# Placing attention keys by small DMAs instead of masked products, with eps as a statistics group and a second shape for the normalise step

## The chip, the cores and the metric

The kernel runs on one core of one Trainium2 chip, in one launch. The metric is the device time in microseconds (us), as the median of several runs. A profile is one execution with tracing, and its *span* runs from the first to the last instruction, about 2 us less than the time of the same execution.

Engines in the profile: PE is TensorE's matmul part, PEld its weight load, DVE is VectorE, ACT is ScalarE, POOL is GpSimd, and SP is SyncE, which here issues every DMA of the program. "SPq" is time in which SP's sequencer executes an instruction.

## The reference, cut to what matters

```python
def _A_ref(x, wqkv, wo):                    # S=2048, D=512, 32 heads of 16, window W=256
    qkv = (x @ wqkv).reshape(B, S, 3, H, Dh).transpose(2, 0, 3, 1, 4)
    q, k, v = qkv[0], qkv[1], qkv[2]
    scores = einsum("bhqd,bhkd->bhqk", q, k) * Dh ** -0.5
    p = softmax(where(causal_and_within_window, scores, -1e9))
    return einsum("bhqk,bhkd->bhqd", p, v)... @ wo
def _B_ref(x, w1, b1, w2, b2):              # F=1792, mixes tokens
    u = gelu(einsum("bsd,sf->bdf", _layernorm(x), w1) + b1)
    return (einsum("bdf,fs->bds", u, w2) + b2).transpose(0, 2, 1)

x = A_x
for _ in range(2):                          # written out twice in the reference
    x = x + _A_ref(_layernorm(x), A_wqkv, A_wo)
    x = x + _B_ref(_layernorm(x), B_w1, B_b1, B_w2, B_b2)
```

Each layernorm is (x - mean) / sqrt(var + 1e-5). B receives a normalised x and normalises it again, so there the two are merged into one.

## The kernel before

The kernel first describes its work as a graph of operations. Then it replays a fixed order, a long packed constant `ORDER` that a scheduler made beforehand: it says which operation stands where, and which of several engines does it. Each engine then runs its own operations strictly in that order. An operation waits on semaphores for what it reads:

```python
for o in self.order[e]:                     # one stream for each engine, SP included
    for s, v in waits[o.idx]:
        eng.wait_ge(sem(s), v)
    ins = o.fn(eng, o.cols32) if o.flex else o.fn(eng)
    ins.then_inc(sem(mark[o.idx][0]), 16 if o.dma else 1)
```

So SP is one queue, in order: the transposed activations (`xhT`), the weights `w1b` and `w2b` of the MLP and everything else stand behind each other, each with its own wait.

Four heads of 16 rows are used at a time by the score matmuls, and two heads share the 32 rows of one such matmul (the profile has all 1488 of them as 32*128). Their keys must therefore lie block-diagonally in `kbd`: for each row group r, rows 32r to 32r+15 hold head 0's keys in one half, and rows 32r+16 to 32r+31 hold head 1's keys in the other, with zeros elsewhere. The kernel before makes this with two products by a 0/1 column `par` for each key tile:

```python
op("vector:evk", lambda e: e.tensor_copy(stg[:, ts.slot, 0:n], at()), ...)   # PSUM to SBUF: "staged"
for h in range(2):
    f_kz = lambda e, h=h: e.tensor_scalar(
        dst(h), stg[:, ts.slot, 0:n].rearrange("p (s n) -> p s n", n=64), par[:, h:h + 1], 0.0,
        op0=ALU.mult, op1=ALU.add)
    op("gpsimd:kz", f_kz, reads=[ts, ("par", h)], ..., alts=[("vector", f_kz, ...)])
```

There are 24 such tiles, 12 in each attention layer (the first block of a layer goes another way). The layernorm:

```python
op("vector:stat", lambda e: e.bn_stats(stats[:, t, :], x_sb[:, t, :]), ...)
op("vector:agg",  lambda e: e.bn_aggr(agg[:, t, :], stats[:, t, :]), ...)
...
op("vector:var",  lambda e: e.tensor_scalar(rstd[:, t0:t1, 0], agg[:, t0:t1, 1], a, b, op0=ALU.mult, op1=ALU.add), ...)
op("gpsimd:rstd", lambda e: e.tensor_tensor(rstd..., rstd..., mhalf..., op=ALU.pow), ...)      # to the power -1/2
op("vector:xh",   lambda e: e.tensor_scalar(xh_sb[:, t, :], x_sb[:, t, :], agg[:, t, 0:1], rstd[:, t, :],
                                            op0=ALU.subtract, op1=ALU.mult), ...)               # "normalise"
```

The softmax here doesn't subtract the row's maximum and nothing guards it: scores larger than these inputs give would overflow.

## Time and profile before

| | before |
|---|---|
| median (lowest to highest) | 464.39 us (460.69 to 464.5) |
| span of the profiled run, mean granted clock | 461.1 us, 0.993 |

The first part of the profile page gives each engine's busy time, its share of the span and its instructions. The fourth part follows the last instruction back through what released it, and gives shares of the span.

```profile
PE 419.1 (91%) x6394; PEld 200.9 (44%) x6456; DVE 323.5 (70%) x596; ACT 325.9 (71%) x377; POOL 226.5 (49%) x296
...
PE 60%; ACT 15%; DVE 11%; POOL 7%; issue 3%; DMA 2%; SPq 1%
```

Next come groups of instructions with equal shapes: engine, operation, what is written and read, count | busy us, mean ns | idle time before them and its main releaser.

```profile
L687 ACT ACTIVATE pt<-PS 128x1024 bf16<-128x1024 f32 x292 | 275.7, 1047 | 24.9 <-PE PS L672 24.0
...
L491 DVE TENSOR_SCALAR xh_sb<-x_sb,agg,rstd 128x512 bf16<-128x512 bf16 x64 | 36.9, 594 | 7.3 <-POOL rstd L484 7.1
...
L595 DVE TENSOR_SCALAR kbd<-stg,par 128x512 bf16<-128x512 bf16 x27 | 15.7, 586 | 0.8 <-ACT stg L593 0.7
L595 POOL TENSOR_SCALAR kbd<-stg,par 128x512 bf16<-128x512 bf16 x21 | 15.5, 739 | 0.0
...
L482 DVE TENSOR_SCALAR rstd<-agg 128x2 f32<-128x2 f32 x31 | 8.8, 285 | 0.5
```

The change aims at the last four: the normalise steps, the key products on two engines, and the small eps steps. Single lines can be asked for their shortest, median and longest duration in ns (then first and last start in us). The three here are a load of weights from HBM by SP, the DMA that transposes activations, and the normalise step:

```profile
L777 SPq DMA_DIRECT2D w1b<-in_B_w_dram x112: 340/469/1679, 44.5 to 401.1; - x112
...
L543 SPq DMA_TRANSPOSE xhT<-xh_sb x24: 1189/1197/2607, 18.1 to 314.1; - x24
...
L491 DVE TENSOR_SCALAR xh_sb<-x_sb,agg,rstd x64: 314/409/1890, 5.2 to 391.6; 128x512 bf16<-128x512 bf16 x64
```

For an SPq line the duration is how long the queue is held, not when the data land: a load of `w1b` holds it for 0.47 us in the median and lands 2.7 us after its issue.

### The profile page before, as it was taken

What the parts mean: (1) busy time and instruction counts of PE and PEld (TensorE: products, weight loads), DVE (VectorE), ACT (ScalarE), POOL (GpSimd) and SP (SyncE); (2) the same over time, 40 slices, a digit from 0 to 9 for tenths busy, and PEclk for the clock granted to TensorE, in tenths of its full rate; (3) what the DMA queues carried; (4) which work ended last, traced back from release to release, by engine and by line L of the source; (5) the groups of instructions that cost most, each with busy time, mean ns of one, the idle gap of its engine ahead of it and who ended that gap; (6) DMA issues with size and microseconds to landing.
All of it is one profiled execution on the core that took longest, in us unless ns stands there. A gap on an engine that the chain in (4) does not pass through costs nothing.

```text
span 461.1 us, 14645 instructions
## 1 busy us (share of the span) xinstructions
PE 419.1 (91%) x6394; PEld 200.9 (44%) x6456; DVE 323.5 (70%) x596; ACT 325.9 (71%) x377; POOL 226.5 (49%) x296
## 2 busy tenths in 40 slices
PE   6998787998777999999999999998789999999996
PEld 5654344354223444445445444434344344444442
DVE  6998799859677649755567867798986698431215
ACT  6998789999988960616988898999979962340000
POOL 3668678677866651000466557676956661000000
PEclk9999999999988999999999999999999999999999
DMA  8412521000040347630063132422003238662443
GB/s 255 134 28 44 134 47 37 3 4 1 25 138 1 103 112 192 172 102 1 15 103 106 13 94 47 117 59 72 3 1 82 72 91 234 181 170 58 134 137 127
DMA packets 82463, 39.76 MB, mean 86 GB/s; under 512 B 20960, under 2 KB 82400, under 8 KB 82400
## 3 DMA queue, kind: packets, MB, share of 16 engines
q1 hardware_dynamic: 82400, 38.82, 32.0%
q8 instruction: 51, 0.84, 0.8%
q14 instruction: 12, 0.10, 0.1%
HBM read 33.56 MB, written 2.10 MB: 77 GB/s over the span
## 4 chain that ended last, share of the span: by engine, by line
PE 60%; ACT 15%; DVE 11%; POOL 7%; issue 3%; DMA 2%; SPq 1%
PE PS L514 35%; ACT pt L687 14%; PE PS L842 8%; POOL pt L705 6%; PE PS L672 6%; PE PS L721 5%; PE PS L609 3%; PE PS L516 3%; DVE rl L741 2%; DVE xh_sb L491 2%; ACT kbd L582 1%; DVE kbd L595 1%; POOL rstd L484 1%; DMA xhT<-xh_sb 1%; DVE qT L572 1%
## 5 line engine op out<-in xcount | busy, mean ns | idle before, releaser
L687 ACT ACTIVATE pt<-PS 128x1024 bf16<-128x1024 f32 (+1 forms) x304 | 283.2, 1036 | 24.9 <-PE PS L672 24.0
L705 POOL TENSOR_TENSOR pt<-pt,ldm 128x256 int32<-128x256 int32 (+3 forms) x216 | 170.7, 805 | 89.7 <-ACT pt L687 83.8
L672 PE MATMUL PS<-qT,kbd 32*128 32x256 bf16 (+4 forms) x1488 | 60.4, 252 | 12.3 <-DVE rl L741 3.0
L514 PE MATMUL PS<-xh_sb,w1b 128*128 128x512 bf16 x256 | 65.2, 385 | 4.4 <-issue 2.5
L514 PE MATMUL PS<-uT,w2b 128*128 128x512 bf16 x257 | 63.2, 380 | 1.7 <-issue 1.3
L869 DVE SCALAR_TENSOR_TENSOR x_sb<-PS,b2col,x_sb 128x512 bf16<-128x512 f32 x32 | 23.5, 748 | 49.7 <-PE PS L514 47.5
L484 POOL TENSOR_TENSOR rstd<-rstd,mhalf 128x2 f32<-128x2 f32 (+1 forms) x33 | 23.9, 725 | 63.8 <-DVE rstd L482 62.4
L721 PE MATMUL PS<-pt,vb 64*32 64x320 bf16 (+4 forms) x2976 | 45.4, 253 | 9.0 <-POOL pt L705 5.4
L741 DVE STREAM_TRANSPOSE rl<-PS 128x1024 f32<-128x1024 f32 x32 | 39.7, 1242 | 17.1 <-PE PS L721 16.8
L514 PE MATMUL PS<-xhT,wqkv 128*128 128x512 bf16 (+1 forms) x198 | 46.4, 356 | 5.4 <-ACT pt L687 2.2
L672 PEld LDWEIGHTS PS<-qT,kbd 32*128 32x128 bf16 x1488 | 21.9, 92 | 67.0 <-ACT pt L687 44.7
L857 ACT ACTIVATE uT<-rl,b1col 128x512 bf16<-128x512 f32 x28 | 18.3, 712 | 42.1 <-DVE rl L853 42.1
L468 DVE BATCH_NORM_STATS2 stats<-x_sb 128x6 f32<-128x512 bf16 x64 | 43.0, 681 | 0.5
L491 DVE TENSOR_SCALAR xh_sb<-x_sb,agg,rstd 128x512 bf16<-128x512 bf16 x64 | 36.9, 594 | 7.3 <-POOL rstd L484 7.1
L721 PEld LDWEIGHTS PS<-pt,vb 64*32 64x32 bf16 x2976 | 28.7, 89 | 27.3 <-POOL pt L705 13.9
L514 PE MATMUL PS<-uT,pt 128*128 128x512 bf16 x165 | 39.8, 379 | 0.2
L514 PEld LDWEIGHTS PS<-xh_sb,w1b 128*128 128x128 bf16 x276 | 23.4, 99 | 33.9 <-issue 8.0
L514 PEld LDWEIGHTS PS<-uT,w2b 128*128 128x128 bf16 x270 | 24.4, 98 | 31.5 <-issue 3.6
L842 PE MATMUL PS<-xh_sb,w1b 128*128 128x512 bf16 x165 | 37.1, 379 | 0.2
L609 PE MATMUL PS<-wqkv,xhT 128*64 128x256 bf16 x512 | 36.0, 276 | 0.7 <-DMA xhT<-xh_sb 0.3
L514 PE MATMUL PS<-wo_sb,oT 128*128 128x512 bf16 x109 | 29.1, 394 | 2.0 <-DVE xh_sb L491 1.0
L609 PEld LDWEIGHTS PS<-wqkv,xhT 128*64 128x64 bf16 x512 | 25.0, 109 | 9.6 <-issue 5.1
(66 smaller groups left out, 380.2 us busy)
## 6 DMA issues: line engine op xcount, KB each, us to landing
w1b<-in_B_w_dram SPq DMA_DIRECT2D x112, 128.0 KB, 2.7
w2b<-in_B_w_dram SPq DMA_DIRECT2D x70, 128.0 KB, 2.5
pt<-in_B_w_dram SPq DMA_DIRECT2D x42, 128.0 KB, 3.1
out_dram<-x_sb SPq DMA_DIRECT2D x16, 128.0 KB, 1.8
x_sb<-in_A_x_dram SPq DMA_DIRECT2D x3, 512.0 KB, 7.5
wqkv<-in_A_wqkv_dram SPq DMA_DIRECT2D x4, 256.0 KB, 4.6
wqkv<-in_A_wqkv_dram SPq DMA_DIRECT2D x1, 512.0 KB, 7.0
wo_sb<-in_A_wo_dram SPq DMA_DIRECT2D x1, 512.0 KB, 4.0
```

What stands on the lines that cost most here:

```text
L468: op("vector:stat", lambda e: e.bn_stats(stats[:, t, :], x_sb[:, t, :]), reads=[f"x{t}"], writes=[f"st{t}"], cost=dve_cost(512), after=lat ...
L484: op("gpsimd:rstd", lambda e: e.tensor_tensor(rstd[:, t0:t1, 0], rstd[:, t0:t1, 0], mhalf[:, 0:1].to_broadcast([P, t1 - t0]), op=ALU.pow), ...
L491: f_xh = lambda e: e.tensor_scalar(xh_sb[:, t, :], x_sb[:, t, :], agg[:, t, 0:1], rstd[:, t, :], op0=ALU.subtract, op1=ALU.mult)
L514: return e.matmul(o, lhsT=w, rhs=x, start=start, stop=stop, skip_group_check=True)
L609: last = e.matmul(bank(ft)[64 * j:64 * j + 64, sc * 256:(sc + 1) * 256], lhsT=xhT[:, tx.slot, c, tok:tok + 64], rhs=wqkv[:, c, 1024:1536]. ...
L672: last = e.matmul(bank(tt[r // 2], r % 2)[:, base + c0 * 64:base + (c0 + n) * 64], lhsT=kbd[32 * r:32 * r + 32, tk.slot, o, jj].rearrange( ...
L687: op("scalar:exp", lambda e, ts=ts, tp=tp, i=i, cols=cols: e.activation(probs(tp)[:, i, 0:cols, :], pair(ts)[:, :, 0:cols].rearrange("p r ...
L705: return e.tensor_tensor(v, v, m, op=ALU.mult)
L721: last = e.matmul(bank(t, h)[32 * r:32 * r + 32, i + q0 * 64:i + (q0 + n) * 64], lhsT=vb[64 * h:64 * h + 64, tk.slot, jj, 4 * o + r, :], r ...
L741: op("vector:od", lambda e, t=tod, tr=tr: e.transpose(rl[:, tr.slot:tr.slot + 2].rearrange("p a b -> p (a b)"), pair(t)), reads=[(tod, i) ...
L842: last = e.matmul(bank(tu, tt), lhsT=v()[:, sc - b0, k0 + tt * P:k0 + (tt + 1) * P], rhs=xh_sb[:, sc, :], start=(sc == b0), stop=(sc == NT ...
L869: op("vector:resy", lambda e: e.scalar_tensor_tensor(x_sb[:, t, :], bank(ft), b2col[:, t:t + 1], x_sb[:, t, :], op0=ALU.add, op1=ALU.add), ...
```

## The change

The intent is to relieve VectorE and GpSimd. A DMA can place the keys, since the off-diagonal zeros stay where they are once written. Eps becomes a third group of statistics, so the aggregate already contains it and the eps step falls away. And half of the normalise steps write 513 elements as three rows of 171, a shape that is meant to keep them from waiting for GpSimd. A new order comes with it, which is not readable as text.

```diff
+        for i in range(1, 3):
+            op("gpsimd:zk", lambda e, i=i: e.memset(kbd[:, i].bitcast(dt.float32), 0.0), reads=["mhalf"], writes=["zk"], ...)
...
-                for h in range(2):
-                    f_kz = lambda e, h=h: e.tensor_scalar(dst(h), stg[...], par[:, h:h + 1], 0.0, ...)
-                    op("gpsimd:kz", f_kz, ..., alts=[("vector", f_kz, ...)])
+                def f_kz(e):
+                    got = []
+                    for h in range(2):
+                        for r in range(4):
+                            p = 32 * r + 16 * h
+                            got.append(e.dma_start(kbd[p:p + 16, tk.slot, o, a // 64:b // 64, h, :],
+                                                   stg[p:p + 16, ts.slot, 0:n].rearrange("p (s n) -> p s n", n=64)))
+                    return got
+                op("sync:kz", f_kz, reads=[ts, "zk"], ..., cost=1500, issue=2000.0, dma=True, parts=8, prio=-2e5)
...
-            op("vector:var", ...)                                   # the eps step
+        op("vector", lambda e: e.memset(stats[:, :, :, 6:9], 0.0), writes=["eps0"])
+        for i, c in enumerate((EPS, EPS * EPS / (1.0 + EPS))):
+            op("vector", lambda e, i=i, c=c: e.memset(stats[:, i, :, 8], D * c), ...)
...
+            def f_xh1(e):                                           # 32 of the 64 normalise steps
+                return e.tensor_scalar(xh_pad[:, t, 0:D + 1].rearrange("p (a b) -> p a b", a=3), x_pad[:, t, 0:D + 1],
+                                       agg[:, t, 0:1], rstd[:, t, :], op0=ALU.subtract, op1=ALU.mult)
...
-    bias=b1col[:, ft:ft + 1], scale=1.0),
+    bias=b1col[:, ft:ft + 1], scale=(1.0 + EPS) ** -0.5),
```

The scheduler's note for a whole group of eight DMAs is `issue=2000.0`, that is 2.0 us of SP.

## The prediction

> **What bounds the kernel now.** No single engine. The busy table gives TensorE 419 of 461 us (91%), ScalarE 326, VectorE 324, GpSimd 227. In the MLP stretches (170 to 215, 381 to 409 us) TensorE is busy 99%. In the two attention layers (9 to 170, 216 to 377 us) the exponentials start every 0.92 us at best: 40 of them need 37 us, and the groups of 40 take 39.7 to 44.8, so ScalarE is nearly full; VectorE is too in places (35 of 40 us from 40 to 80, 37 of 40 from 300 to 340, where TensorE idles 6 to 8 us). The chain of waits says the same: PE 60%, ACT 15%, DVE 11%, POOL 7%. TensorE's idle time, 42 us, caps the gain.
>
> **What the change removes.** The key products: 27 on VectorE (15.7 us, 586 ns each), 21 on GpSimd (15.5 us); 33 epsilon steps on VectorE (9.1 us). The new order takes a net 6 evictions from ScalarE (0.6 us each). The normalise step has minimum 314, median 409, mean 594 and maximum 1890 ns: such a tail is a wait. [...]
>
> **What it adds.** 192 DMAs of 16 partitions, in 24 groups of eight, on the one SP queue; two zero fills of about 1.9 us; 9 instead of 6 statistics per aggregate (166 ns, near unchanged). A plain issue takes 332 to 469 ns in the trace, so I estimate 2.7 to 3.5 us per group, 72 us in all. SP waited some 300 us before, so it has room, but it is in order. The packets are 128 B; 256 B ones took 18 ns, so moving them costs about 5% of the DMA engines: no limit.
>
> **How much is critical.** VectorE sheds about 20 us plus lock waits, GpSimd 14. Most is off the chain: its "normalise" and "key product" pieces were 3% (14 us). ScalarE sheds 3 to 4 us in its full stretches. Gain: 8 to 12 us. Against it: a key tile now passes staging (0.7), eight issues (3) and landing (2), about 6 us, where the order leaves 5 to 7 us of TensorE work between the key matmuls and the first scores in about four places: 2 to 4 us of score stalls. Net about 8 us: **456.5 us**, 8 in 10 between 448 and 464. Faster by over 2%: 0.40; within 2%: 0.55; slower by over 2%: 0.05.
>
> **What would show it.** VectorE busy near 300 us, GpSimd near 210; [...]groups of 40 exponentials falling toward 39 us; eight issues per key tile near 3 us; a few waits of score matmuls on the key DMA, up to 2 us; MLP stretches unchanged.
>
> **What would make it wrong.** Issues of 16-partition DMAs costing clearly more than 0.4 us, which delays transposes and weight loads behind them; or far less, when the gain reaches 12 us. The new order removing stalls beyond those named, such as the 3.6 us wait for a weight load at 442 us and the half-clock spell at 143 us.

The sum is: 8 to 12 us gained, 2 to 4 lost in score stalls, net about 8 and so 456.5 us. The "lock waits" stand in it, without a figure of their own.

What those waits are the trace before does show. The 24 normalise steps with no GpSimd operation beside them take 314 to 414 ns. Of the 40 others, 17 take 367 to 416 ns and 23 take 509 to 1890, and each of these 23 ends 0.15 us after the end of a mask or key product on GpSimd.

## More of the kernel before

TensorE is busy for 91% of the span, and DMA is almost absent from the chain: hardly any data is waited for.

No plain copy between two on-chip buffers stands in this trace. The view of waits for SP, then the one for all other engines (total us, times, longest):

```profile
SPq L777 <- PE PS L672: 85.5, 6, 49.6
```

```profile
PEld PS L514 <- DMA w2b<-in_B_w_dram: 0.6, 1, 0.6
```

SP is mostly waiting: the line shown, its largest, is weight loads that wait for their buffer. And TensorE practically never waits for a DMA: the second line is its largest such wait.

## The result, and the profile after

| | before | after |
|---|---|---|
| median of 4 runs each, side by side | 464.44 us | 494.94 us (493.52 to 497.17) |
| span, granted clock | 461.1 us, 0.993 | 491.4 us, 0.964 |

The ratio is 1.068, with a 95% interval of 1.061 to 1.075: slower by 7%, and outside the predicted range. Ratios here are the mean time of one kernel's fast runs over the mean of the other's fast runs of the same rounds, so they are not quite the ratio of the medians quoted.

The page of the kernel after:

```profile
PE 428.8 (87%) x6376; PEld 204.1 (42%) x6438; DVE 313.0 (64%) x547; ACT 322.9 (66%) x371; POOL 212.0 (43%) x275
...
PE 57%; ACT 11%; DVE 9%; POOL 8%; SPq 7%; DMA 4%; issue 3%; POOLq 0%
```

Each engine that was to be relieved has less to do, yet the span is 30 us longer. SPq and DMA are now 11% of the chain, from 3%. The lines of the new DMAs, of the weight loads and of the two normalise forms:

```profile
L613 SPq DMA_DIRECT2D kbd<-stg x192: 585/600/1830, 41.2 to 381.4; - x192
...
L795 SPq DMA_DIRECT2D w1b<-in_B_w_dram x112: 340/469/1881, 54.2 to 431.6; - x112
...
L504 DVE TENSOR_SCALAR xh_pad<-x_pad,agg,rstd x32: 371/448/1981, 6.0 to 422.0; 128x513 bf16<-128x513 bf16 x32
...
L500 DVE TENSOR_SCALAR xh_pad<-x_pad,agg,rstd x32: 371/520/1865, 6.8 to 421.2; 128x512 bf16<-128x512 bf16 x32
```

A 16-partition DMA between on-chip buffers holds SP for 0.60 us and never less than 0.585, against the 0.34 to 0.44 that the prediction's 2.7 to 3.5 us per eight imply; weight loads cost what they did. The two normalise forms are told apart by one element, and both have a tail near 1.9 us. What TensorE waits for, in the view of waits:

```profile
PE PS L690 <- DMA kbd<-stg: 8.0, 3, 5.6
...
PEld PS L527 <- DMA xhT<-xh_pad: 6.9, 1, 6.9
...
PEld PS L529 <- DMA xhT<-xh_pad: 5.2, 1, 5.2
...
PEld PS L527 <- DMA w2b<-in_B_w_dram: 5.0, 2, 3.3
...
PEld PS L527 <- DMA w1b<-in_B_w_dram: 3.3, 1, 3.3
```

These sum to 28.4 us in eight waits, where before they were 1 us. (A late DMA appears on PEld and again on PE; I count the PEld line, and the PE line for the keys.) Less than a third of it is for the keys. The rest is for activations and weights that the change did not touch. The timeline of SP shows why; its columns are start, duration, instruction and count:

```profile
90.86 11.32 SPq L613 DMA_DIRECT2D kbd<-stg  x16
102.23 1.27 SPq L556 DMA_TRANSPOSE xhT<-xh_pad  x1
```

And the chain of work of the kernel after, in order of time, passes through this very place:

```profile
90.86 0.64 SPq L613
...
91.54 0.60 SPq L613
...
101.59 0.60 SPq L613
...
102.23 2.50 DMA xhT<-xh_pad
...
104.78 1.89 PE PS L527 x4
```

Two groups of eight hold SP for 11.3 us. A transpose stands behind them, and TensorE gets its activations 2.5 us after that.

Where the 30 us went, by stretch. The columns are: the start of the first exponential; then from the first exponential of one block of queries to that of the next (c0 to c3); the last block with the first MLP; the same in the second layer (c3' ends with the last exponential); and the rest. A full block has 40 large exponentials. All from the profiled runs, in us:

| | start | c0 | c1 | c2 | c3 | MLP 1 | c0' | c1' | c2' | c3' | rest |
|---|---|---|---|---|---|---|---|---|---|---|---|
| before | 9.7 | 12.8 | 21.7 | 42.9 | 39.7 | 89.2 | 34.7 | 44.8 | 39.9 | 41.2 | 84.6 |
| after | 14.2 | 12.4 | 22.5 | 46.1 | 46.9 | 89.6 | 36.8 | 53.1 | 41.9 | 44.7 | 83.2 |

The MLP stretches are as before. The loss lies in the attention blocks into which key groups are issued, and 4.5 us of it at the start. (Three groups are issued in the stretch "MLP 1", which begins with the layer's last attention block, and cost next to nothing there.) There the timeline of the kernel after (start, duration, engine, operation, and in brackets the idle time before it) has

```profile
6.72 1.80 POOL L460 MEMSET kbd<- 128x2048 f32 x1
...
6.80 1.86 DVE L500 TENSOR_SCALAR xh_pad<-x_pad,agg,rstd 128x512 bf16<-128x512 bf16 x1 [0.45 <-POOL rstd L492]
```

while before it had

```profile
6.05 0.41 DVE L491 TENSOR_SCALAR xh_sb<-x_sb,agg,rstd 128x512 bf16<-128x512 bf16 x1 [0.46 <-POOL rstd L484]
```

GpSimd's zero fill started 0.08 us before the second normalise step and lasts 1.80, and the step ends 0.15 us after the fill, as the 23 long steps of the kernel before end after a mask or a product: 1.86 us behind the fill, 0.41 without it. The first of the two fills stretches another VectorE step in the same way (L447, 0.88 us; 0.22 in the kernel before). These two waits are 2.1 of the 4.5 us. TensorE's clock also stood at half from 9.15 to 12.57 us, as it did not at the start of the kernel before or of the run "All tiles by DMA, late fills" below; the rest is not traced.

### The profile page after: what moved, and what is told of

Its sections match the earlier page's. It is cut to its first block, busy times and chain, and to the rows that moved or that the text cites. A ratio compares the mean times of both kernels' runs of the same rounds, so it can differ in the third digit from the quotient of the medians.

```text
span 491.4 us, 14733 instructions
## 1 busy us (share of the span) xinstructions
PE 428.8 (87%) x6376; PEld 204.1 (42%) x6438; DVE 313.0 (64%) x547; ACT 322.9 (66%) x371; POOL 212.0 (43%) x275
## 4 chain that ended last, share of the span: by engine, by line
PE 57%; ACT 11%; DVE 9%; POOL 8%; SPq 7%; DMA 4%; issue 3%; POOLq 0%
PE PS L527 32%; ACT pt L705 11%; PE PS L860 7%; POOL pt L723 7%; SPq L613 6%; PE PS L690 5%; PE PS L739 5%; PE PS L627 4%; PE PS L529 3%; DMA xhT<-xh_pad 1%; DVE xh_pad L500 1%; DMA w2b<-in_B_w_dram 1%; DVE stats L479 1%; POOL rstd L492 1%; DVE rl L759 1%
## 5 line engine op out<-in xcount | busy, mean ns | idle before, releaser
L723 POOL TENSOR_TENSOR pt<-pt,ldm 128x256 int32<-128x256 int32 (+2 forms) x216 | 171.6, 811 | 113.7 <-ACT pt L705 110.6
L690 PE MATMUL PS<-qT,kbd 32*128 32x256 bf16 (+4 forms) x1488 | 61.8, 256 | 15.5 <-DMA kbd<-stg 8.0
L527 PE MATMUL PS<-xh_pad,w1b 128*128 128x512 bf16 x258 | 65.3, 382 | 9.3 <-DMA w1b<-in_B_w_dram 2.8
L492 POOL TENSOR_TENSOR rstd<-agg,mhalf 128x2 f32<-128x2 f32 (+1 forms) x33 | 23.4, 708 | 90.2 <-DVE agg L481 90.1
L527 PE MATMUL PS<-xhT,wqkv 128*128 128x512 bf16 (+1 forms) x215 | 52.5, 377 | 10.1 <-DMA xhT<-xh_pad 6.4
L759 DVE STREAM_TRANSPOSE rl<-PS 128x1024 f32<-128x1024 f32 x32 | 39.7, 1241 | 25.6 <-PE PS L739 25.6
L887 DVE SCALAR_TENSOR_TENSOR x_pad<-PS,b2col,x_pad 128x512 bf16<-128x512 f32 x32 | 23.4, 746 | 48.1 <-PE PS L527 45.6
L739 PE MATMUL PS<-pt,vb 64*32 64x320 bf16 (+4 forms) x2976 | 46.1, 256 | 5.3 <-POOL pt L723 3.8
L875 ACT ACTIVATE uT<-rl,b1col 128x512 bf16<-128x512 f32 x28 | 18.2, 712 | 40.9 <-DVE rl L871 40.9
L479 DVE BATCH_NORM_STATS2 stats<-x_pad 128x6 f32<-128x512 bf16 x64 | 42.7, 677 | 0.5
L527 PE MATMUL PS<-uT,pt 128*128 128x512 bf16 x164 | 40.3, 379 | 0.2
L627 PE MATMUL PS<-wqkv,xhT 128*64 128x256 bf16 x512 | 38.6, 288 | 1.5 <-ACT pt L705 0.8
L527 PEld LDWEIGHTS PS<-xh_pad,w1b 128*128 128x128 bf16 x276 | 23.0, 98 | 38.6 <-issue 7.6
L860 PE MATMUL PS<-xh_pad,w1b 128*128 128x512 bf16 x165 | 37.4, 379 | 0.2
L527 PEld LDWEIGHTS PS<-xhT,wqkv 128*128 128x128 bf16 x232 | 20.9, 103 | 31.4 <-issue 7.7
L638 DVE CAST vb<-PS 128x512 bf16<-128x512 f32 x30 | 20.2, 679 | 20.7 <-PE PS L627 20.7
L627 PEld LDWEIGHTS PS<-wqkv,xhT 128*64 128x64 bf16 x512 | 26.1, 114 | 12.1 <-issue 6.1
```

The source lines that it names most:

```text
L479: op("vector:stat", lambda e: e.bn_stats(st[:, 0:6], x_sb[:, t, :]), reads=[f"x{t}"], writes=[("st", i)], cost=dve_cost(512), after=late_s ...
L492: op("gpsimd:rstd", lambda e: e.tensor_tensor(rstd[:, t0:t1, 0], agg[:, t0:t1, 1], mhalf[:, 0:1].to_broadcast([P, t1 - t0]), op=ALU.pow), ...
L527: return e.matmul(o, lhsT=w, rhs=x, start=start, stop=stop, skip_group_check=True)
L627: last = e.matmul(bank(ft)[64 * j:64 * j + 64, sc * 256:(sc + 1) * 256], lhsT=xhT[:, tx.slot, c, tok:tok + 64], rhs=wqkv[:, c, 1024:1536]. ...
L690: last = e.matmul(bank(tt[r // 2], r % 2)[:, base + c0 * 64:base + (c0 + n) * 64], lhsT=kbd[32 * r:32 * r + 32, tk.slot, o, jj].rearrange( ...
L723: return e.tensor_tensor(v, v, m, op=ALU.mult)
```

## The experiments

The theory after the result: 24 groups of eight issues at 0.64 us each (0.60 and a gap of 0.04) take 5.1 us a group, 123 us in all, of an in-order queue; what stands behind a group comes late, and TensorE waits. The rivals: the new order itself is poor; the queue is simply too full; the DMAs' data moves or lands too slowly; the keys alone are late; the other parts (eps, normalise, fills) cost the time. "Before" in each ratio is the kernel before in the same rounds; its medians there were 462.3 to 464.1 us. Four kernels give a wrong result; all others were correct. Unless said otherwise, each edit is to the kernel after and the order is its own, with only the changed operations put in or taken out.

### One DMA of eight (wrong result)

```diff
-                    for h in range(2):
-                        for r in range(4):
+                    for h in range(1):
+                        for r in range(1):
```

> The changed kernel, but each key tile is placed by one of its eight DMAs only (wrong result on purpose; same kind of DMA, same order, same fills). The trace of the change shows 0.60 us for one issue and 0.64 us from one issue to the next, so a group holds the SP queue for 5.1 us. Queue theory: the loss outside the start-up is SP in-order time; a group falls to 0.6 us, so of the 30 us lost, all but the 4.5 us of the start-up come back or more: 455 to 470 us, with no waits of matmuls on key or weight DMAs above 1 us. Order theory (the new sequence on the compute engines is worse whatever the DMAs cost): at most a third comes back, 483 to 495 us.

Measured: 461.25 us, ratio 0.998 (0.993 to 1.003). The order is the new one, and seven eighths of the issues are gone: so is the loss. The seven additional DMAs per tile cost 494.94 - 461.25, about 34 us. The view of waits no longer lists any wait of TensorE for a DMA. The new order as such is not the cause.

### Four DMAs of eight (wrong result)

```diff
-                    for h in range(2):
+                    for h in range(1):
```

> As before but four of the eight DMAs (wrong result on purpose). Queue theory: a group takes 2.6 us, near the 2.0 us that the change itself writes down for it, so most comes back: 460 to 476 us; and if the loss were proportional to queue time, halfway between one and eight (about 478). A threshold near the written 2.0 us shows as four lying much nearer to one than to eight. Order theory: 488 to 495 us.

Measured: 461.6 us, ratio 0.998 (0.993 to 1.002), no slower than with one. So the cost is not proportional to the number of DMAs: groups of 2.6 us are hidden, groups of 5.1 us cost 34 us. TensorE's waits for any DMA, of which nothing over 0.8 us is left:

```profile
PE PS L682 <- DMA kbd<-stg: 0.8, 1, 0.8
PEld PS L519 <- DMA w1b<-in_B_w_dram: 0.7, 1, 0.7
PEld PS L519 <- DMA xhT<-xh_pad: 0.3, 1, 0.3
```

Each issue still takes 0.60 us in the median. What differs is the lag from a key staged to its last issue: in the median 13.9 us with eight, 7.6 with four, 4.5 with one.

### Products back in the new kernel

```diff
-                op("sync:kz", f_kz, reads=[ts, "zk"], ..., dma=True, parts=8)
+                op("gpsimd:kz", f_kz, reads=[ts, ("par", h), "zk"], ..., alts=[("vector", f_kz, ...)])   # twice, as before
```

> The changed kernel with the key products back on VectorE and GpSimd (the same engine for each as before the change), everything else kept: new order, epsilon group, 513-wide normalise, zero fills. Right result. Queue theory: SP is free again, so 460 to 475 us (start-up loss of 4.5 us kept, the order was not made for this load). Order theory: 485 us or more.

Measured: 472.7 us, ratio 1.021 (1.016 to 1.025). The DMAs go and 22 us come back. What remains above before is, by the stretches, the price of the early fills, which are kept here (the first exponential starts at 14.5 us), and of products in an order that was not made for them: c2' takes 42.8 us instead of 39.9, and the stretch "MLP 1" 92.2 instead of 89.2.

### DMAs in the old kernel

```diff
 (the kernel before, its order)
-                op("gpsimd:kz", f_kz, ..., alts=[("vector", f_kz, ...)])        # two products
+                op("sync:kz", f_kz, reads=[ts, "zk"], ..., dma=True, parts=8)   # eight DMAs, as in the change
+        two fills of kbd, in slots where GpSimd was idle
```

> The kernel before, in its own order, with only the keys changed: eight DMAs per tile at the place of the first key product, the two zero fills put where GpSimd was idle. Right result. Queue theory: the old order leaves SP as little room, so the loss appears without any other part of the change: 480 to 505 us. Order theory: the DMAs are harmless, 460 to 470 us.

Measured: 515.1 us, ratio 1.113 (1.107 to 1.119). In the old order, DMAs in place of products cost 52 us, more than the 22 us between the two in the new order, although the start is as before (9.7 us). The DMAs lose time in either order; the new order even softens them. TensorE's waits for DMAs are 47 us here, 17.4 of them for `w2b` alone.

### Two tiles in one DMA

```diff
-                got.append(e.dma_start(kbd[p:p + 16, tk.slot, o, ...], stg[p:p + 16, ts.slot, ...]))
+                got.append(e.dma_start(kbd[p:p + 16, tk.slot, o0:o0 + n0, ...], stg[p:p + 16, ts.slot:ts.slot + n0, ...]))
```

Twenty of the 24 tiles go two at a time, which makes 112 DMAs of 192.

> The changed kernel, but 20 of the 24 key tiles are placed two at a time: the same eight 16-partition DMAs carry two tiles (16 runs of 128 B in each partition instead of 8), so 14 groups instead of 24 and 112 DMAs instead of 192. Right result. Queue theory with a fixed cost for each DMA (0.60 us whatever it carries): 72 us of queue instead of 122, in bursts of 5.1 us as before but fewer: 464 to 476 us. If the issue time grows with the runs (1.0 us or more for one): 480 us or more.

Measured: 494.54 us, ratio 1.067 (1.062 to 1.071): no gain, a miss for the theory in its simple form, in which the number of issues decides. The profile shows what took its place. A DMA holds SP for 609 ns in the median, with twice the data as with once. But the pair now waits in the queue for the second tile, and everything behind it waits too. The view of SP's waits:

```profile
SPq L611 <- DVE stg L598: 28.9, 4, 10.4
...
SPq L611 <- DVE w2b L845: 18.6, 1, 18.6
```

In the kernel after, the key DMAs' waits on the same producers were 12.7 and 13.9 us. The test is confounded: it trades issue time against waiting at the head of the queue, and cannot tell how much either weighs.

### Two tiles in one DMA, and late fills

```diff
-   reads=["mhalf"]
+   reads=["mhalf", "xh0", "xh1"]      # the two fills come after the first two normalise steps
```

> As pairs, and the two zero fills on GpSimd wait for the first two normalise steps instead of running beside them. If the fills cause the start-up loss by keeping VectorE out[...], the first exponential starts at about 11.5 us instead of 14.2 to 14.5 and the kernel is 2 to 4 us faster than pairs. If the start-up loss is the new order of VectorE's set-up steps, under 1 us.

Measured: 489.4 us, ratio 1.056 (1.052 to 1.060), 5 us less than without the late fills. The first exponential starts at 10.8 us instead of 15.5. Most of the start loss is the fills' doing; 1.1 us over the 9.7 of the kernel before stays.

### Only the eps part, in the kernel before

```diff
-        stats = sb("stats", [P, NT, 6], dt.float32)
+        stats = sb("stats", [P, 2, 8, 9], dt.float32)
-            op("vector:var", ...)
```

and the memsets and the gelu scale of the change.

> The kernel before in its own order, with only the epsilon moved into a third statistics group (33 small VectorE steps of 285 ns gone, statistics rows of 9). Right result. If this part helps by itself: 1 to 3 us faster (VectorE is nearly full in two stretches); if it is off the chain: within 0.5 us of the kernel before.

Measured: 460.51 us, ratio 0.993 (0.991 to 0.995), five rounds. This small part helps by 0.7% alone. It is the best correct version and beats both kernels, though by less than 2%.

### Six forms of the key DMA (wrong result)

One DMA for each tile, in six shapes in turn, to measure what an issue depends on:

```diff
+                    if form == 0: return e.dma_start(d8[0:16], s8[0:16])   # 16 partitions, 8 runs each
+                    if form == 1: return e.dma_start(d1[0:16], s1[0:16])   # 16 partitions, 1 run each
+                    if form == 2: return e.dma_start(d8[0:32], s8[0:32])
+                    if form == 3: return e.dma_start(d8[0:64], s8[0:64])
+                    if form == 4: return e.dma_start(d8, s8)               # 128 partitions, 8 runs each
+                    return e.dma_start(d1, s1)                             # 128 partitions, 1 run each
```

> Wrong result on purpose: one DMA for a key tile, of six forms in turn, to measure the issue. 16 partitions of 8 runs of 128 B (as in the change), 16 of one run of 1 KB, 32, 64 and 128 partitions of 8 runs, 128 partitions of one run. If the issue is a fixed cost of a DMA between two on-chip tiles: all near 0.6 us. If it follows the number of runs: the one-run forms of 16 partitions well under 0.5 us, 128 x 8 runs over 1 us. Time about 461 us as with one DMA.

One look, 461.45 us, state unknown. The six lines in the order of the six forms, with shortest, median and longest ns:

```profile
L607 SPq DMA_DIRECT2D kbd<-stg x4: 605/674/1452, 41.6 to 300.3; - x4
L609 SPq DMA_DIRECT2D kbd<-stg x4: 562/587/598, 52.2 to 287.7; - x4
L611 SPq DMA_DIRECT2D kbd<-stg x4: 632/672/682, 52.9 to 323.6; - x4
L613 SPq DMA_DIRECT2D kbd<-stg x4: 650/666/688, 43.1 to 336.5; - x4
L615 SPq DMA_DIRECT2D kbd<-stg x4: 642/662/680, 65.1 to 337.9; - x4
L616 SPq DMA_DIRECT2D kbd<-stg x4: 497/556/1677, 85.4 to 338.6; - x4
```

The medians lie between 0.56 and 0.67 us, from 16 to 128 partitions and from one to eight runs each. An issue between on-chip buffers cost about 0.6 us in each of these forms. Neither the 16 partitions nor the short packets make it dear, but the count does: eight of them. With four samples of each form, no finer order among them is claimed.

### Each group cut in two

Each group of eight becomes two operations of four, the second behind the next two operations of SP.

```diff
-                op("sync:kz", f_kz, ..., parts=8)
+                for h in range(2):
+                    op("sync:kz", f_kz, ..., parts=4)
```

> The changed kernel with every group of eight DMAs cut into two groups of four, the second put behind the next two transposes or weight loads of the queue (but ahead of the scores that need it). Right result; queue time in all unchanged, 122 us, in bursts of 2.6 us. One, four and eight DMAs gave 461, 462 and 495 us, and pairing tiles (72 us of queue in bursts of 5.1) gave 494.5. If the length of a burst in front of a needed transfer is what costs: 465 to 480 us. If the filling of the queue in the busy stretches costs: 488 us or more.

Measured: 496.01 us, ratio 1.071 (1.067 to 1.074). No gain. c3 gains (42.4 us instead of 46.9), but c2 loses as much (50.8 instead of 46.1): a transpose gets through earlier, and the second half of a key comes later, as I read it. The issue time is still all there; SP is issuing for 92% of c2. But the edit is no clean test of shorter bursts: halves of neighbouring groups came to lie together, and in SP's timeline 112 of the 192 DMAs still go out in bursts of eight or twelve, four of them in c2.

### Half by DMA, half by product, late fills

```diff
-                    for h in range(2):
-                        for r in range(4):
+                    for r in range(4):                                   # head 0 by four DMAs
+                op("gpsimd:k1", f_k1, ..., alts=[("vector", f_k1, ...)])   # head 1 by one product
```

> The changed kernel with the first head of each pair placed by four DMAs and the second by the old product on VectorE or GpSimd (24 in place of 48 products), and the zero fills behind the first two normalise steps. Right result. Queue theory: the queue is as short as with four DMAs (461.6 us), the start-up loss of 4.7 us goes, 24 products come back: 456 to 464 us, better than or equal to the kernel before. If the products are what the order cannot bear (all 48 gave 472.7 with the early fills): 464 to 470 us.

Measured: 462.64 us, ratio 0.997 (0.994 to 0.9997), five rounds, correct. This is what the four-DMA run promised, now with a right result: from +6.8% to -0.3% by halving the DMAs, with 24 of the 48 products back, and moving the fills. TensorE's waits for DMAs are 2.7 us.

### The same with rows that stay apart (wrong result)

In the built program of the kernel after, the three rows of 171, which touch, are one run of 513. Here the three rows get a pitch of 172, which puts elements in wrong places (one small memset fills the gaps at the start):

```diff
-   e.tensor_scalar(xh_pad[:, t, 0:D + 1].rearrange("p (a b) -> p a b", a=3), ...
+   e.tensor_scalar(xh_pad[:, t, 0:516].rearrange("p (a b) -> p a b", a=3)[:, :, 0:171], ...
```

> As hybrid_late, but the 32 normalise steps[...] write three rows of 171 at a pitch of 172, so that the rows cannot be merged into one run of 513 as they are in the trace of the change (wrong result on purpose: the columns are shifted). [...] If the shape changes nothing: same durations and tail as in the change.

Measured: 459.4 us, ratio 0.991 (0.988 to 0.994), five rounds: 0.6% faster than the run before it, in the same rounds. The line of these 32 steps (shortest, median, longest; its form 128x513 counts elements and is printed alike for both runs, but the trace's record of the operands has a destination of 513 in the kernel after and of 171 x 3 here):

```profile
L495 DVE TENSOR_SCALAR xh_pad<-x_pad,agg,rstd x32: 496/534/545, 5.5 to 389.2; 128x513 bf16<-128x513 bf16 x32
```

The tail is gone: 545 ns at most, against 1981 in the kernel after, and against 1364 for the other 32 steps (128x512) of this same run. At its best it is slower (496 against 371 ns), and its mean is lower (529 ns, against 619 in the run with touching rows). So the shape decides: 513 to 513 elements ran at the 371 ns of the 128x512 form at their shortest and waited for GpSimd; 3 rows of 171 with a gap against 513 took 0.53 us and never showed a wait of that kind. Why it does is not shown here. 1.6 us of the 3 us gain lies in the start-up.

### The DMAs issued by GpSimd

```diff
-                op("sync:kz", f_kz, ..., dma=True, parts=8)
+                op("gpsimd:kz", f_kz, ..., dma=True, parts=8)      # with semaphores of its own, and late fills
```

> The changed kernel with all eight DMAs of each group issued from the GpSimd queue in place of SP, and the late fills. Right result. Queue theory: SP's transposes and weights are on time again; if an issue costs GpSimd under 0.2 us, 455 to 468 us; if it costs about 1 us, GpSimd loses 190 us, its masks come late and the kernel takes over 500 us.

Measured: 547.33 us, ratio 1.180 (1.176 to 1.184), the slowest of all. The line of the DMAs and the chain:

```profile
L602 POOL DMA_DIRECT2D kbd<-stg x192: 528/528/721, 40.0 to 439.4; - x192
```

```profile
PE 46%; POOL 33%; ACT 12%; DVE 4%; issue 2%; DMA 1%; SPq 0%; POOLq 0%
```

192 issues of 0.53 us are 101 us more on an engine whose masks stand between the exponentials and the value matmuls; POOL is now 33% of the chain. The time on the issuing engine does not go away with the queue: it is 0.53 us on GpSimd, 0.60 on SP.

### All tiles by DMA, late fills

```diff
-   reads=["mhalf"]
+   reads=["mhalf", "xh0", "xh1"]
```

> The changed kernel, complete, with the two zero fills behind the first two normalise steps and nothing else altered. Right result. Upper end of the next three: all 24 tiles by eight DMAs. If the fills cost the start-up its 4.7 us and the gain is kept: 489 to 492 us. If the queue takes it back later, since it is full in the third stretch whatever the start: 492 to 496 us.

Measured: 490.32 us, ratio 1.059 (1.055 to 1.064). The late fills give back about 4 us: 4.6 between the medians, which come from different rounds, and 5.9% over before instead of 6.8%. The first exponential starts at 10.8 us instead of 14.2 and c0 takes 11.0 instead of 12.4; each later stretch is within 2 us of the kernel after. TensorE's waits for DMAs, to be compared with the reordered run below:

```profile
PE PS L679 <- DMA kbd<-stg: 8.4, 3, 6.0
...
PEld PS L516 <- DMA xhT<-xh_pad: 6.1, 1, 6.1
...
PEld PS L516 <- DMA w2b<-in_B_w_dram: 5.0, 2, 3.2
...
PEld PS L518 <- DMA xhT<-xh_pad: 4.6, 1, 4.6
...
PEld PS L516 <- DMA w1b<-in_B_w_dram: 3.2, 1, 3.2
```

### No tile by DMA, late fills

```diff
+                both products for all 24 tiles, in the order of the kernel after
```

> As dma_all, but all 24 tiles by the products on VectorE and GpSimd. Right result. Lower end: 472.7 with the early fills, so 467 to 470 us with the late ones.

Measured: 470.06 us, ratio 1.015 (1.012 to 1.018). It is the other end of the scale for the next two. Its waits for DMAs are 0.4 us.

### Only part of the tiles by DMA

Ten tiles have their DMAs issued in the two stretches where SP was fullest, c2 and c1' (SP issuing for 98% and 83% of the time, from 39% and 28% before). "Slack" does these ten by products and the other 14 by DMAs; "busy" does the reverse.

```diff
+                if 12 * layer + 4 * (m - 1) + o in (1, 2, 4, 5, 6, 13, 14, 15, 16, 19):    # slack; busy: the others
+                    ... the two products ...
+                    return
```

> As dma_all, but the ten tiles whose DMAs are issued in the two stretches where the SP queue is fullest in the trace of the change (98% from 49 to 95 us, 83% from 268 to 321 us) are made by the products; the other 14 tiles keep eight DMAs each. Right result. If a full queue costs and a burst of 5.1 us in a queue with room does not: 462 to 471 us. If every burst costs alike: 14/24 of the way from dma_none to dma_all, about 480 us.

> The reverse: those ten tiles by eight DMAs, the other 14 by the products. Right result. If a full queue costs: within 6 us of dma_all, 484 to 494 us. If every burst costs alike: 10/24 of the way, about 477 us.

Measured: slack 471.46 us, ratio 1.018 (1.014 to 1.022); busy 472.56 us, ratio 1.020 (1.016 to 1.025).

| | start | c0 | c1 | c2 | c3 | MLP 1 | c0' | c1' | c2' | c3' | rest |
|---|---|---|---|---|---|---|---|---|---|---|---|
| none | 10.8 | 12.1 | 23.6 | 44.4 | 40.1 | 92.2 | 35.0 | 43.3 | 42.8 | 40.9 | 83.2 |
| slack | 10.8 | 12.4 | 22.5 | 47.4 | 39.8 | 90.8 | 36.9 | 42.9 | 39.7 | 44.7 | 82.6 |
| busy | 10.8 | 11.0 | 23.0 | 40.9 | 40.3 | 92.2 | 35.0 | 48.5 | 45.0 | 40.9 | 82.6 |
| all | 10.8 | 11.0 | 22.9 | 46.9 | 46.7 | 91.5 | 36.9 | 53.3 | 41.4 | 44.7 | 83.2 |

The full queue as such is not the cause: in "busy", SP issues for 99% of c2, and c2 takes 40.9 us, less than without any DMA. The stalls do not add up either. Over "none", slack is 1.4 us longer, busy 2.5, all 20.3. Part of this is that every tile by DMA also takes two products away. The one-DMA run suggests about 9 us for all 24 (470.06 - 461.25, early fills notwithstanding); an estimate that divides this by tiles makes the stalls 6.5, 6.2 and 29 us. With some 4 us more for that run's early fills it makes them 9, 8 and 33. Either way all is about twice the sum of its parts or more. c3 shows it: 39.8 and 40.3 us with a part of the groups, 46.7 with all. SP's timeline says why. In "all", two groups stand in front of one transpose, and one is of each half; with a part of the groups, one of the two is left. The burst in front of that transpose in all, slack and busy:

```profile
87.05 10.75 SPq L602 DMA_DIRECT2D kbd<-stg  x16
...
85.88 5.29 SPq L611 DMA_DIRECT2D kbd<-stg  x8
...
81.38 6.03 SPq L612 DMA_DIRECT2D kbd<-stg  x8
```

TensorE then waits 6.1 us for the transpose in all, not at all in slack and 1.9 us in busy. A late operation is harmless until the slack of a block is used up, and then it stops TensorE. Not all of the loss needs both halves: c1' takes 48.5 us in busy (43.3 in none), and c3' 44.7 in slack, as in all (40.9 in none).

### Only SP's order changed

All tiles by DMA and late fills. In SP's queue, 37 transposes and weight loads that stood directly behind a group of eight are moved ahead of it. No other engine's order is changed.

```diff
 (order of SP alone)
- ... eight key DMAs, transpose or weight load ...
+ ... transpose or weight load, eight key DMAs ...
```

> As dma_all (490.3 us: all 24 tiles by eight DMAs, late fills), the compute engines' order untouched, but in the order of the SP queue 37 transposes and weight loads that in the trace of dma_all went out without a wait straight behind a group of eight are put in front of that group (transposes only where their input was ready; not in front of the six groups whose scores come soonest). Right result; 192 DMAs and 122 us of queue time as before. If the loss is a handful of needed transfers that stand behind a group: most of the 20 to 30 us comes back, 466 to 478 us, and the waits of TensorE for transposes and weights of 3 to 6 us are gone. If the queue time itself is what costs: 486 us or more.

Measured: 476.93 us, ratio 1.028 (1.026 to 1.031), against 490.32 for the same kernel without the moves (the two ran in different rounds, with medians of before of 464.05 and 462.31). By the ratios the excess over before falls from 5.9% to 2.8%: about half of it, 13 to 15 us, was time behind the groups. c3 takes 39.2 us instead of 46.7 and c1' 47.2 instead of 53.3, while c2 stays at 47.1. TensorE's waits:

```profile
PE PS L679 <- DMA kbd<-stg: 13.2, 5, 5.8
...
PEld PS L516 <- DMA w1b<-in_B_w_dram: 2.9, 1, 2.9
...
PEld PS L516 <- DMA xhT<-xh_pad: 0.8, 1, 0.8
PEld PS L516 <- DMA w2b<-in_B_w_dram: 0.6, 1, 0.6
```

The waits for transposes and weights fall from 18.9 to 4.3 us, and those for the keys rise from 8.4 to 13.2. The sum falls by 9.8 us, from 27.3 to 17.5, and the time by 13.4. What remains is mainly the keys themselves, which come 5.1 us of issues and 1.9 us of landing after their turn. This rearrangement does not remove that; fewer issues did.

## Why the prediction was wrong, point by point

**The step that failed.** "A plain issue takes 332 to 469 ns in the trace, so I estimate 2.7 to 3.5 us per group, 72 us in all." It was carried over from loads out of HBM and stores to it to copies between on-chip buffers, of which the trace before had none; its one DMA between on-chip buffers, the transpose, took 1.2 us, which should have been a warning. Measured: 600 ns, 0.64 from issue to issue, 5.1 us per group, 123 us in all. The note in the change itself, 2.0 us per group, is off by more. An issue cost this much in all six forms tried.

**The step that followed from it.** "SP waited some 300 us before, so it has room, but it is in order", and then "2 to 4 us of score stalls". The room was real on average and useless where groups of eight come in a row: two of them hold the queue for 11.3 us. The prediction counted only the keys' own path as critical, and five of the eight TensorE waits, 20 of 28 us, were for transposes and weights behind the groups. A cost of 2 to 4 us was in truth about 34. The section on what would make it wrong did name this, issues clearly above 0.4 us that delay transposes and weight loads, but gave it almost no weight: 5% for slower.

**The gain was of the right size where it could show.** With one DMA per tile the span is 457.7 us, 3.4 less than before, with 4.8 lost at the start: about 8 us gained elsewhere, as predicted ("Gain: 8 to 12 us"). GpSimd's busy time is 212.0 us (predicted near 210). VectorE's is 313.0, not near 300: 24.8 us of products and eps steps went, but its busy time fell by 10.5 only. The groups show about 10 us that came back: some 7 of evictions and divisions that the order gave it, 1.2 of the larger aggregates (166 to 181 ns each), 1.6 of the normalise steps (36.9 to 38.5 us in all); the rest I did not trace. The groups of 40 exponentials do come down with one DMA per tile, to between 39.1 and 41.4 us in c2, c3 and c1' to c3'; in the kernel after they take 41.9 to 53.1.

**The start was missed.** The two fills were priced, at 1.9 us (each took 1.80), but not placed. They held up VectorE in the first microseconds, where everything hangs on one normalise step. Late fills gave back 5 us in the same rounds (the pairs), about 4 in the kernel after.

**The shape in three rows never came to be.** A passage expected these 32 steps to lose their tail and the masks to be shorter. The tail stayed (1981 ns): the steps have the shortest duration of the 128x512 form (371 ns) and a median of 448 with waits in it, while the separated rows take 534. The masks were no shorter (the commonest form took 750 ns before and 744 after, two others 1284 and 1313, 469 and 475). The three touching rows are one run of 513. The built program has them as one run, so this could have been seen without running it. The separated rows do behave as the change meant its own to: 545 ns at most.

**Right as predicted:** the MLP stretches are unchanged (89.2 and 89.6; 84.6 and 83.2 us); moving the data is no limit: the landing time is 1.9 us, and the 24,576 packets of 128 B took 11 ns each in the median. The key waits of the score matmuls were few, three, but up to 5.6 us, not 2. (The prediction's "3.6 us wait for a weight load at 442 us" was read off the chain, where it is the load's own time; in the view of waits TensorE waited 0.6 us for it.)

**What stays open.** The clock. TensorE is busy 9.7 us longer for the same matmuls, and the trace after has about 34 us at half clock in seven spells of 3.41 or 6.83 us, where before it had two spells of 3.41 us (a spell that begins in the last microsecond or after the end is left out). In the 3.41 us before each of these nine, TensorE was busy for at most 1.78 us; but from 43.1 to 46.5 us of the kernel before it was busy for 1.71, and no spell followed. That stalls are amplified by the clock is therefore my guess: the span grows by 30.3 us, the waits for DMAs by 27.4, and the granted clock is 0.964, against 0.992 with one DMA per tile. No run separated the two. What uses up the slack of c3 is shown, the transpose behind two groups; the other blocks were not taken apart in this way.

## What to carry to other kernels

Price a DMA by what it holds its queue for, measured for the same kind of source and target, and multiply by the count (here 0.34 us at the shortest and 0.47 in the median for a load from HBM, medians of 0.56 to 0.67 for a copy between on-chip buffers, 1.2 for a transposing DMA); when it serves a just-in-time pipeline, look at what stands behind it in the in-order queue, not at the queue's average idle time. Moving work off a busy engine pays only while the new path fits into the slack of a block, and beyond that the loss can be steep: four DMAs per tile were free here, eight cost 34 us, and nothing between was run. Put one-time fills where no urgent step of VectorE stands beside them (here 1.86 us beside a fill, 0.41 without), and check in the built instructions that an access pattern is still the one you wrote.
